# Full products written as four 32-column strips in the runs that hold value products

## The chip, the cores and the metric

The kernel runs on one core of a Trainium2 chip. Its time is the device time of that core in microseconds (us); the time before is the median of three runs. TensorE (PE in the profile) multiplies, VectorE (DVE), ScalarE (ACT) and GpSimd (POOL) work on what it leaves in PSUM and in SBUF, and SyncE (SP) issues most transfers. The profile is that of one execution.

## The reference

One input x of 2048 rows of 512 numbers goes through two branches, which a gate mixes row by row.

```python
qkv = (x @ wqkv).reshape(B, S, 3, 32, 16)           # 32 heads of 16
scores = einsum("bhqd,bhkd->bhqk", q, k) * 16 ** -0.5
mask = (i - j >= 0) & (i - j < 256)                 # a sliding window
a = (softmax(where(mask, scores, -1e9)) @ v) @ wo
b = (silu(x @ w1) * (x @ w3)) @ w2                  # F = 1376
g = sigmoid((x * gate_w).sum(-1))
out = g * a + (1 - g) * b
```

## The kernel before

TensorE's products come in three forms, by the part of the 128 x 128 array that one of them uses.

- *Full* products use 128 rows and 128 columns: the projections of q and k (`chain`, L422) and of v (`vmm`, L499), the up products of the second branch (`half`, L825, and `mm_b`, L785), its down products (`part`, L875) and the output product (`omm`, L905). A full product with 512 moving columns is the common one; those of v have 128 or 129, those of L785 have 64.
- *Row* products are the scores. A head pair's keys fill 32 of the 128 rows; four products for four row groups stand side by side (`main_batch`, L560: 8 products of 256 columns; `edge_batch`, L610: 32 products of 64 columns).
- *Column* products are the value products, in which the exponentials are multiplied by v (`pv`, L700). Each uses 128 rows and 17 columns (16 of v and one of ones for the sum); four of them write the four quarters of 32 partitions of one PSUM buffer. There are 16 blocks of them, for 4 groups of heads (c) and 4 parts of 512 query rows (w), each in two passes, and each pass needs a PSUM buffer.

PSUM holds one buffer `su` of four banks for scores and four buffers `ch_0` to `ch_3` of one bank for everything else. A buffer `ch` is free again when the instruction that reads it out is done. For the up products these are a tanh on ACT (L835) and two multiplications on DVE (L839, L845); q is copied by DVE (L480), k copied (L459) and then masked in two halves (L465) and copied once more (L462), v copied (L512) and shifted by POOL (L517). Exponentials run on ACT (L564, L614); POOL cuts their masked triangles to zero (L569, L574, L627) and DVE does part of the edge tiles (L633, L637). The result of the value products is transposed, normalised and transposed back by DVE (L724, L727, L730, L734). The down products are scaled by DVE (L880), and DVE joins both branches (L909) ahead of the output transfer (L915).

Nothing at run time chooses the order. The class `Plan` holds all operations, each with an engine, an estimated duration, the operations that it depends on, the buffers that it takes and frees, and a due time. `emit` walks them once on the host: of the engines it takes the one that can start first, and on it, among the operations that could start then, the one with the smallest rank, which is the due time. The order in which the operations leave `emit` is the order in each engine's queue, and every engine works its queue strictly in that order, waiting on semaphores. The due times come from some thirty numbers in the table `K` (L230), such as when the k projection of a part is due (`LEAD`) or the value products (`PV`).

Two parts of `emit` bear on forms. When the form of the next TensorE operation differs from the form before it, the estimated start is put back by `SWITCH` = 0.117 us. And `rank` (L70) moves due times by form: a row or column operation behind another that is not full gets 0.265 earlier (`ADJ`), a column operation behind a full one 1.114 later (`SEP`).

Of the kernel before, what the change touches and what calls it, by code (L numbers as in the profile page):

```python
# [15 lines left out]
P = 128  # L16
# [4 lines left out]

PIPE = {"DVE": 0.105, "ACT": 0.112, "POOL": 0.045}
LAT = {"PE": 0.205}
SWITCH = 0.117


class Op:
    __slots__ = ("eng", "dur", "lat", "fn", "deps", "due", "take", "free", "seq", "start", "end", "slots", "hold", "form")

    def __init__(self, eng, dur, fn, deps, due, take, free, lat, seq, form):  # L30
        self.eng, self.dur, self.fn, self.due, self.lat, self.seq = eng, dur, fn, due, lat, seq
        self.deps = [d for d in deps if d is not None]
        self.take, self.free = take, free
        self.start = self.end = None
        self.hold = 0.0
        self.form = form


class Job:
# [6 lines left out]
class Plan:  # L46


    def __init__(self, slots, beside, apart):
        self.ops = []  # L50
        self.slots = slots
        self.beside, self.apart = beside, apart

    def add(self, eng, dur, fn, deps=(), due=0.0, take=(), free=(), lat=None, form="full"):
        if lat is None:
# [5 lines left out]
    def pieces(self, cuts, each, fn, deps, due, take, lat=None, free=()):  # L61
# [4 lines left out]
                            [prev] if prev else deps, due, take=take if lo == 0 else (),  # L66
                            free=free if hi == cuts[-1] else (), lat=lat)
        return prev

    def rank(self, op, form):  # L70
        due = op.due
        if op.eng == "PE" and op.form != "full":
            if form != "full":
                due -= self.beside
            elif op.form == "column":
                due += self.apart
        return due, op.seq

    def emit(self):
        free_at = {k: [0.0] * n for k, n in self.slots.items()}  # L80
        holders = {}
        for op in self.ops:
            for job, kind in op.free:
                holders.setdefault((id(job), kind), [0, 0.0])[0] += 1
        engine = {}
        form = "full"
        todo = {}
        users = {}
        for op in self.ops:
            todo[op.seq] = len(op.deps)  # L90
            for d in op.deps:
                users.setdefault(d.seq, []).append(op)
        ready = [op for op in self.ops if not op.deps]
        order = []
        while ready:
            best = None
            lists = {}
            for op in ready:
                est = engine.get(op.eng, 0.0)
                for d in op.deps:  # L100
                    e = d.end if d.eng != op.eng else d.start + d.dur + (0.03 if op.eng in PIPE else 0.0)
# [12 lines left out]
            if first > 1e8:  # L114
                raise RuntimeError("no free buffer")
            rows = [r for r in lists[eng] if r[0] <= first + 0.001]
            held = [r for r in lists[eng] if r[1].hold and r[0] <= first + r[1].hold]
            est, op = min(held or rows, key=lambda r: self.rank(r[1], form))
            if eng == "PE" and op.form != form:
                est = max(est, engine.get(eng, 0.0) + SWITCH)  # L120
                form = op.form
            for job, kind in op.take:
                i = min(range(len(free_at[kind])), key=lambda j: free_at[kind][j])
                free_at[kind][i] = 1e9
                job.at[kind] = i
            op.start = est
            op.end = est + op.dur + op.lat + SLACK
            engine[op.eng] = est + op.dur - PIPE.get(op.eng, 0.0)
            for job, kind in op.free:
                h = holders[(id(job), kind)]  # L130
                h[0] -= 1
                h[1] = max(h[1], op.end)
                if h[0] == 0:
                    free_at[kind][job.at[kind]] = h[1]
            ready.remove(op)
            for u in users.get(op.seq, ()):
                todo[u.seq] -= 1
                if todo[u.seq] == 0:
                    ready.append(u)
            order.append((est, op))  # L140
        assert len(order) == len(self.ops)
        self.order = order
        for est, op in order:
            op.fn()


@with_exitstack
def kernel(
# [12 lines left out]
    nc = tc.nc  # L161
# [12 lines left out]
    FB = FL - FA  # L174
# [20 lines left out]
    hT = pp.tile([P, NFC - 1, 512], BF16, name="hT")  # L195
# [30 lines left out]
    ot = [pp.tile([P, D], BF16, name=f"ot_{i}") for i in range(4)]  # L226
    su = ps.tile([P, 4, 512], F32, name="su")
    ch = [ps.tile([P, 512], F32, name=f"ch_{i}") for i in range(4)]

    K = {"T0": 6.663, "TA": 234.789, "TF0": -1.359, "TF1": 251.583, "PV": 0.213, "EDGE": -2.966, "HOLD": -4.301, "LEAD": 9.863, "QLEAD": -3.864, "V": 5.26, "O0": -0.819, "O1": 5.827, "O2": 6.852, "O3": 24.592, "FE": -3.084, "PE": -2.787, "VE": -3.291, "MK": 4.4, "UP": 2.598, "_km": 1.0, "_lo": 1.0, "LE": 4.467, "ADJ": 0.265, "SEP": 1.114, "BE": -2.825}  # L230
    plan = Plan({"su": 1, "ch": 4, "Em": len(Em), "Ee": len(Ee), "kt": 2, "tt": 2, "h1": 2,
                 "tn": len(tn), "ot": len(ot), "hT": 1},
                K["ADJ"], K["SEP"])
    add = plan.add


    def half_of(base, a):
# [167 lines left out]
    def projections(c, tq):  # L405
# [13 lines left out]
        def chain(job, col, lo, hi, t0=0, t1=512):  # L419
            pst = ch[job.at["ch"]]  # L420
            for dc in range(lo, hi):
                nc.tensor.matmul(pst[:, t0:t1], lhsT=wqkv_sb[:, dc, col + c * P:col + (c + 1) * P],  # L422
                                 rhs=xT[:, dc, tq * 512 + t0:tq * 512 + t1],
                                 start=(dc == 0), stop=(dc == NDC - 1))

# [62 lines left out]
        for m0, nm in ([(4 * tq, 2), (4 * tq + 2, 2)] if c == 0 else [(4 * tq, 4)]):  # L488
# [3 lines left out]
            def vmm(lo, hi, vj=vj, m0=m0, w=w):  # L492
                pst = ch[vj.at["ch"]]
                for mm in range(lo, hi):
                    m = m0 + mm
                    for dc in range(NDC):
                        rhs = (wv0[:, dc, 0:w] if c == 0
                               else wqkv_sb[:, dc, 2 * D + c * P:2 * D + (c + 1) * P])
                        nc.tensor.matmul(pst[:, mm * w:(mm + 1) * w], lhsT=xT[:, dc, m * P:(m + 1) * P],  # L499
                                         rhs=rhs, start=(dc == 0), stop=(dc == NDC - 1))  # L500

            def v_of(rows, base, a, m0=m0, nm=nm):
# [268 lines left out]
    for tcb in range(NTC):  # L771
# [3 lines left out]
        def tail_columns(tcb=tcb):  # L775
# [4 lines left out]
            def mm_b():  # L780
                po = ch[job.at["ch"]]
                for mm in range(4):
                    m = 4 * tcb + mm
                    for dc in range(NDC):
                        nc.tensor.matmul(po[:, mm * 2 * FB:(mm + 1) * 2 * FB], lhsT=xT[:, dc, m * P:(m + 1) * P],  # L785
                                         rhs=wB[:, dc, :], start=(dc == 0), stop=(dc == NDC - 1))

            def cols(lo):
# [26 lines left out]
        for f in range(NFC):  # L815
# [6 lines left out]

            def half(job, w, lo, hi, f=f, joint=joint, tcb=tcb):
                for dc in range(lo, hi):
                    nc.tensor.matmul(ch[job.at["ch"]][:],  # L825
                                     lhsT=wA[:, dc, :] if joint else w[:, dc, f * P:(f + 1) * P],
                                     rhs=xT[:, dc, tcb * 512:(tcb + 1) * 512],
                                     start=(dc == 0), stop=(dc == NDC - 1))
# [36 lines left out]
        for mm in range(4):  # L865
# [4 lines left out]
            def part(f0, f1, job=job, mm=mm, tcb=tcb):  # L870
                bps = ch[job.at["ch"]]
                for f in range(f0, f1):
                    fs = P if f < NFC - 1 else FL
                    ht = hT[:, f] if f < NFC - 1 else hX[0:FL, tcb % 2]
                    nc.tensor.matmul(bps[:], lhsT=ht[:, mm * P:(mm + 1) * P],  # L875
                                     rhs=w2_sb[0:fs, f, :], start=(f == 0), stop=(f == NFC - 1))

            def bev(job=job, m=m):
# [18 lines left out]
    def output(m, n0, n1, queue, late):  # L897
# [4 lines left out]
        def omm(lo, hi):  # L902
            pso = ch[job.at["ch"]]
            for c in range(lo, hi):
                nc.tensor.matmul(pso[:, 0:part], lhsT=OT[:, c, m * P:(m + 1) * P], rhs=wo_sb[:, c, n0:n1],  # L905
                                 start=(c == 0), stop=(c == NDC - 1))

        def oev():
# [60 lines left out]
```

## Time and profile before

| | us |
|---|---|
| median of three runs | 240.12 (239.61 to 240.42) |
| the profiled execution, its own time | 240.56 |
| span of the profiled execution | 238.8 |
| TensorE busy (matmul rows) | 231.3 |
| DVE busy | 201.3 |
| ACT busy | 171.2 |
| POOL busy | 159.6 |

The span runs from the first instruction to the last on the core; the execution's own time holds 1.8 us more around it. A busy time is the union of an engine's rows. TensorE's rows overlap, since a product's row ends only when its result has drained, so a busy TensorE isn't TensorE at its peak: what one product costs is read from the starts of two that follow each other. A row of a group reads: line, engine, operation, what is written and read, shapes, how often; then busy us and mean ns of one; then the idle time of the engine ahead of it, and what ended it. In a timeline row the first two numbers are the start and the length, in us, of a group of like instructions that stand together. The granted clock of TensorE is 1.000 over the whole span.

### The profile page before, as it was taken

To read this page: it belongs to the slowest core of one execution; us is meant where nothing else is said; L and a number is where in the kernel's file an instruction comes from. 1 tells how busy PE (TensorE), PEld (TensorE's weight loads), DVE (VectorE), ACT (ScalarE), POOL (GpSimd) and SP (SyncE) were. 2 spreads that over 40 slices of the span, in tenths; PEclk is the share of its full clock that TensorE was granted. 3 is DMA by queue.
4 is the path that set the end of the run, shared out by engine and by line. 5 is a ranking of instruction groups with operands and counts; after the bars stand their busy time and mean duration, and the time that the engine had idled before them with its cause. 6 is when DMAs were issued, how large, how long until landed. Compare 5 with 4: busy or idle time off the path is not lost.

```text
span 238.8 us, 8528 instructions
## 1 busy us (share of the span) xinstructions
PE 231.3 (97%) x3738; PEld 118.8 (50%) x3738; DVE 201.3 (84%) x342; ACT 171.2 (72%) x141; POOL 159.6 (67%) x261
## 2 busy tenths in 40 slices
PE   8999999999999999999989899999999999999994
PEld 8554544546463543545454544545454545445442
DVE  5576998967699989996699999987899897969885
ACT  3389798876867898666858788776768989766510
POOL 7259967979857877587475777768494968575500
PEclk9999999999999999999999999999999999999999
DMA  7999980000000000000000000000000001002133
GB/s 199 205 335 276 201 212 17 5 1 3 3 3 0 5 11 11 7 0 3 3 3 3 1 8 20 3 0 3 3 3 5 3 0 25 3 22 69 52 108 110
DMA packets 20413, 11.59 MB, mean 49 GB/s; under 512 B 9656, under 2 KB 20376, under 8 KB 20376
## 3 DMA queue, kind: packets, MB, share of 16 engines
q1 hardware_dynamic: 19680, 10.59, 17.7%
q8 instruction: 29, 0.48, 0.9%
q10 hardware_dynamic: 696, 0.46, 0.6%
q14 instruction: 8, 0.07, 0.1%
HBM read 6.85 MB, written 2.10 MB: 37 GB/s over the span
## 4 chain that ended last, share of the span: by engine, by line
PE 72%; DVE 19%; ACT 4%; issue 2%; POOL 1%; DVEq 0%; ACTq 0%
PE ch L825 20%; PE ch L875 15%; PE ch L422 9%; PE ch L700 8%; PE su L560 6%; PE ch L905 5%; PE ch L499 4%; ACT Ee L614 4%; DVE h L839 3%; PE su L610 2%; DVE Ee L633 2%; DVE hT L845 2%; DVE Ee L637 2%; DVE tn L724 2%; DVE k L465 2%
## 5 line engine op out<-in xcount | busy, mean ns | idle before, releaser
L564 ACT ACTIVATE Em<-su 128x2048 bf16<-128x2048 f32 x60 | 112.6, 1877 | 34.6 <-PE su L560 31.4
L825 PE MATMUL ch<-xT,w_sb 128*128 128x512 bf16 x320 | 79.3, 380 | 0.5 <-DVE vs L512 0.3
L569 POOL TENSOR_SCALAR_AFFINE_SELECT Em<-Em 64x512 bf16<-64x512 bf16 x60 | 41.1, 685 | 32.5 <-ACT Em L564 26.9
L627 POOL TENSOR_SCALAR_AFFINE_SELECT Ee<-Ee 64x1024 bf16<-64x1024 bf16 x32 | 42.7, 1333 | 21.4 <-ACT Ee L614 19.3
L825 PEld LDWEIGHTS <-w_sb 128*128 128x128 bf16 x320 | 28.4, 98 | 34.8 <-issue 6.9
L875 PE MATMUL ch<-w_sb,hT 128*128 128x512 bf16 x160 | 40.3, 380 | 0.0
L574 POOL TENSOR_SCALAR_AFFINE_SELECT Em<-Em 64x512 bf16<-64x512 bf16 x56 | 37.3, 665 | 3.2
L614 ACT ACTIVATE Ee<-su 128x2048 bf16<-128x2048 f32 x16 | 30.0, 1876 | 10.3 <-PE su L610 7.6
L422 PE MATMUL ch<-xT,wqkv_sb 128*128 128x512 bf16 (+1 forms) x136 | 34.3, 372 | 0.0
L517 POOL COPY vs<-vs 64x256 bf16<-64x256 bf16 (+1 forms) x80 | 30.6, 382 | 5.1 <-DVE vs L512 1.8
L839 DVE SCALAR_TENSOR_TENSOR h<-tt,ch 128x512 bf16<-128x512 bf16 (+1 forms) x44 | 29.6, 677 | 4.7 <-ACT tt L835 4.5
L845 DVE SCALAR_TENSOR_TENSOR hT<-h,ch 128x512 bf16<-128x512 bf16 x40 | 27.1, 677 | 1.9
L835 ACT ACTIVATE tt<-ch 128x512 bf16<-128x512 f32 (+1 forms) x44 | 25.7, 594 | 2.4 <-PE ch L825 2.2
L700 PEld LDWEIGHTS <-vs 128*17 128x17 bf16 x1664 | 21.1, 92 | 8.6 <-issue 6.3
L700 PE MATMUL ch<-Em,vs 128*17 128x256 bf16 (+2 forms) x672 | 22.9, 242 | 2.4 <-DVE h L839 1.7
L700 PE MATMUL ch<-Ee,vs 128*17 128x64 bf16 x992 | 22.6, 193 | 0.0
L875 PEld LDWEIGHTS <-hT 128*128 128x128 bf16 x160 | 13.9, 98 | 16.8 <-issue 3.2
L422 PEld LDWEIGHTS <-wqkv_sb 128*128 128x128 bf16 x136 | 12.4, 99 | 12.7 <-issue 2.1
L499 PEld LDWEIGHTS <-xT 128*128 128x128 bf16 x256 | 15.8, 97 | 5.6 <-issue 1.8
L880 DVE TENSOR_SCALAR bsb<-ch,omg 128x512 bf16<-128x512 f32 x15 | 11.2, 747 | 7.6 <-PE ch L875 7.4
L560 PE MATMUL su<-qT,kz 32*128 32x256 bf16 x240 | 17.3, 278 | 0.2
L560 PE MATMUL su<-qT,k 32*128 32x256 bf16 x240 | 16.7, 268 | 0.0
(81 smaller groups left out, 257.4 us busy)
## 6 DMA issues: line engine op xcount, KB each, us to landing
out_dram<-ot SPq DMA_DIRECT2D x15, 128.0 KB, 1.7
wqkv_sb<-in_A_wqkv_dram SPq DMA_DIRECT2D x5, 256.0 KB, 5.7
w_sb<-in_B_w_dram SPq DMA_DIRECT2D x1, 1280.0 KB, 6.7
w_sb<-in_B_w_dram SPq DMA_DIRECT2D x2, 608.0 KB, 7.8
w_sb<-in_B_w_dram SPq DMA_DIRECT2D x2, 512.0 KB, 5.2
w_sb<-in_B_w_dram SPq DMA_DIRECT2D x2, 256.0 KB, 4.9
wo_sb<-in_A_wo_dram SPq DMA_DIRECT2D x1, 512.0 KB, 5.5
xs<-in_A_x_dram SPq DMA_DIRECT2D x1, 256.0 KB, 2.9
```

The costliest lines, as they stand in the source:

```text
L422: nc.tensor.matmul(pst[:, t0:t1], lhsT=wqkv_sb[:, dc, col + c * P:col + (c + 1) * P], rhs=xT[:, dc, tq * 512 + t0:tq * 512 + t1], start=(d ...
L560: nc.tensor.matmul(su[:, s, a * 256:(a + 1) * 256], lhsT=head_keys(r, t, a), rhs=qT[r, q0:q0 + 256], start=True, stop=True)
L564: nc.scalar.activation(out=Em[job.at["Em"]][:], in_=su[:].rearrange("p s (a q) -> p s a q", a=2), func=ACT.Exp, scale=SCALE)
L569: nc.gpsimd.affine_select(out=e, in_=e, pattern=[[0, 8], [1, KB]], compare_op=ALU.is_ge, fill=0.0, base=0, channel_multiplier=-1)
L574: nc.gpsimd.affine_select(out=e, in_=e, pattern=[[0, 8], [-1, KB]], compare_op=ALU.is_ge, fill=0.0, base=-1, channel_multiplier=1)
L614: nc.scalar.activation(out=Ee[ej.at["Ee"]][:].rearrange("p s t k q -> p s (t k q)"), in_=su[:], func=ACT.Exp, scale=SCALE)
L627: nc.gpsimd.affine_select(out=e, in_=e, pattern=[[0, 4], [0, 4], [1, KB]], compare_op=ALU.is_ge, fill=0.0, base=0, channel_multiplier=-1)
L700: nc.tensor.matmul(po[32 * s:32 * s + VW, lo - 512 * w:hi - 512 * w], lhsT=vs[:, i, a * VW:(a + 1) * VW], rhs=mov, start=(n == 0), stop=(n ...
L825: nc.tensor.matmul(ch[job.at["ch"]][:], lhsT=wA[:, dc, :] if joint else w[:, dc, f * P:(f + 1) * P], rhs=xT[:, dc, tcb * 512:(tcb + 1) * 512],
L839: nc.vector.scalar_tensor_tensor(out=h1[job.at["h1"]][ru, :], in0=tt[job.at["tt"]][rg, :], scalar=1.0, in1=ch[job.at["ch"]][rg, :], op0=AL ...
L845: nc.vector.scalar_tensor_tensor(out=dst, in0=h1[job.at["h1"]][ru, :], scalar=0.5, in1=ch[up.at["ch"]][ru, :], op0=ALU.mult, op1=ALU.mult)
L875: nc.tensor.matmul(bps[:], lhsT=ht[:, mm * P:(mm + 1) * P], rhs=w2_sb[0:fs, f, :], start=(f == 0), stop=(f == NFC - 1))
```

## The change

Every full product that the plan issues, transposes apart, goes through a new function `product`, which writes it in one of two ways.

```diff
+    def product(out, lhsT, rhs, start, stop):
+        if not plan.strips:
+            nc.tensor.matmul(out, lhsT=lhsT, rhs=rhs, start=start, stop=stop)
+            return
+        for j in range(0, P, 32):
+            nc.tensor.matmul(out[j:j + 32], lhsT=lhsT[:, j:j + 32], rhs=rhs, start=start, stop=stop)
```

Where `plan.strips` is set, the 128 columns of the weights are cut into four strips of 32; each strip multiplies the same moving columns and writes a quarter of the partitions. Which operations are written so is decided after the order is known: TensorE's operations are cut into runs between row operations, and every operation of a run that holds a column operation is marked.

```diff
+        run = []
+        for op in [op for est, op in order if op.eng == "PE"] + [None]:
+            if op and op.form != "row":
+                run.append(op)
+                continue
+            column = any(o.form == "column" for o in run)
+            for o in run:
+                o.strips = column
+            run = []
         for est, op in order:
+            self.strips = op.strips
             op.fn()
```

The order is computed anew as well. A change of form is charged only where one side is a row operation, at 0.125 instead of 0.117 us; `rank` and its two numbers are gone; and the numbers of `K` are others.

```diff
-SWITCH = 0.117
+SWITCH = 0.125
...
-            est, op = min(held or rows, key=lambda r: self.rank(r[1], form))
-            if eng == "PE" and op.form != form:
-                est = max(est, engine.get(eng, 0.0) + SWITCH)
+            est, op = min(held or rows, key=lambda r: (r[1].due, r[1].seq))
+            if eng == "PE":
+                if op.form != form and "row" in (op.form, form):
+                    est = max(est, engine.get(eng, 0.0) + SWITCH)
                 form = op.form
...
-    K = {"T0": 6.663, "TA": 234.789, "TF0": -1.359, "TF1": 251.583, "PV": 0.213, "EDGE": -2.966, "HOLD": -4.301, "LEAD": 9.863, "QLEAD": -3.864, "V": 5.26, "O0": -0.819, "O1": 5.827, "O2": 6.852, "O3": 24.592, "FE": -3.084, "PE": -2.787, "VE": -3.291, "MK": 4.4, "UP": 2.598, "_km": 1.0, "_lo": 1.0, "LE": 4.467, "ADJ": 0.265, "SEP": 1.114, "BE": -2.825}
+    K = {"T0": 6.766, "TA": 235.106, "TF0": -1.288, "TF1": 251.005, "PV": 0.365, "EDGE": -3.423, "HOLD": -4.941, "LEAD": 10.494, "QLEAD": -3.881, "V": 6.91, "O0": -1.457, "O1": 6.08, "O2": 6.573, "O3": 24.217, "FE": -2.851, "PE": -2.787, "VE": -3.545, "MK": 5.885, "UP": 2.958, "_km": 1.0, "_lo": 1.0, "LE": 5.367, "BE": -3.541}
```

The products at L422, L499, L785, L825, L875 and L905 call `product` in place of `nc.tensor.matmul`, with the same arguments. In the program that results, 214 full products are written as strips and 822 as before. Instructions that other engines execute are the same in number and kind, in another order.

More of the change, by code (lines that the diff above doesn't have):

```diff
@@ L23 @@
 LAT = {"PE": 0.205}
-SWITCH = 0.117
+SWITCH = 0.125
 class Op:
-    __slots__ = ("eng", "dur", "lat", "fn", "deps", "due", "take", "free", "seq", "start", "end", "slots", "hold", "form")
+    __slots__ = ("eng", "dur", "lat", "fn", "deps", "due", "take", "free", "seq", "start", "end", "slots", "hold", "form", "strips")
     def __init__(self, eng, dur, fn, deps, due, take, free, lat, seq, form):
@@ L36, in __init__ @@
         self.form = form
+        self.strips = False
 class Job:
@@ L46, with __init__ @@
 class Plan:
-    def __init__(self, slots, beside, apart):
+    def __init__(self, slots):
         self.ops = []
         self.slots = slots
-        self.beside, self.apart = beside, apart
+        self.strips = False
     def add(self, eng, dur, fn, deps=(), due=0.0, take=(), free=(), lat=None, form="full"):
@@ L68, in pieces @@
         return prev
[L70 to L77, printed above, removed]
     def emit(self):
@@ L228 @@
     ch = [ps.tile([P, 512], F32, name=f"ch_{i}") for i in range(4)]
-    K = {"T0": 6.663, "TA": 234.789, "TF0": -1.359, "TF1": 251.583, "PV": 0.213, "EDGE": -2.966, "HOLD": -4.301, "LEAD": 9.863, "QLEAD": -3.864, "V": 5.26, "O0": -0.819, "O1": 5.827, "O2": 6.852, "O3": 24.592, "FE": -3.084, "PE": -2.787, "VE": -3.291, "MK": 4.4, "UP": 2.598, "_km": 1.0, "_lo": 1.0, "LE": 4.467, "ADJ": 0.265, "SEP": 1.114, "BE": -2.825}
+    K = {"T0": 6.766, "TA": 235.106, "TF0": -1.288, "TF1": 251.005, "PV": 0.365, "EDGE": -3.423, "HOLD": -4.941, "LEAD": 10.494, "QLEAD": -3.881, "V": 6.91, "O0": -1.457, "O1": 6.08, "O2": 6.573, "O3": 24.217, "FE": -2.851, "PE": -2.787, "VE": -3.545, "MK": 5.885, "UP": 2.958, "_km": 1.0, "_lo": 1.0, "LE": 5.367, "BE": -3.541}
     plan = Plan({"su": 1, "ch": 4, "Em": len(Em), "Ee": len(Ee), "kt": 2, "tt": 2, "h1": 2,
-                 "tn": len(tn), "ot": len(ot), "hT": 1},
-                K["ADJ"], K["SEP"])
+                 "tn": len(tn), "ot": len(ot), "hT": 1})
     add = plan.add
+    def product(out, lhsT, rhs, start, stop):
[4 more added lines that the diff above has]
+            nc.tensor.matmul(out[j:j + 32], lhsT=lhsT[:, j:j + 32], rhs=rhs, start=start, stop=stop)
     def half_of(base, a):
@@ L421, in chain @@
             for dc in range(lo, hi):
-                nc.tensor.matmul(pst[:, t0:t1], lhsT=wqkv_sb[:, dc, col + c * P:col + (c + 1) * P],
+                product(pst[:, t0:t1], lhsT=wqkv_sb[:, dc, col + c * P:col + (c + 1) * P],
                                  rhs=xT[:, dc, tq * 512 + t0:tq * 512 + t1],
@@ L498, in vmm @@
                                else wqkv_sb[:, dc, 2 * D + c * P:2 * D + (c + 1) * P])
-                        nc.tensor.matmul(pst[:, mm * w:(mm + 1) * w], lhsT=xT[:, dc, m * P:(m + 1) * P],
+                        product(pst[:, mm * w:(mm + 1) * w], lhsT=xT[:, dc, m * P:(m + 1) * P],
                                          rhs=rhs, start=(dc == 0), stop=(dc == NDC - 1))
@@ L784, in mm_b @@
                     for dc in range(NDC):
-                        nc.tensor.matmul(po[:, mm * 2 * FB:(mm + 1) * 2 * FB], lhsT=xT[:, dc, m * P:(m + 1) * P],
+                        product(po[:, mm * 2 * FB:(mm + 1) * 2 * FB], lhsT=xT[:, dc, m * P:(m + 1) * P],
                                          rhs=wB[:, dc, :], start=(dc == 0), stop=(dc == NDC - 1))
@@ L824, in half @@
                 for dc in range(lo, hi):
-                    nc.tensor.matmul(ch[job.at["ch"]][:],
+                    product(ch[job.at["ch"]][:],
                                      lhsT=wA[:, dc, :] if joint else w[:, dc, f * P:(f + 1) * P],
@@ L874, in part @@
                     ht = hT[:, f] if f < NFC - 1 else hX[0:FL, tcb % 2]
-                    nc.tensor.matmul(bps[:], lhsT=ht[:, mm * P:(mm + 1) * P],
+                    product(bps[:], lhsT=ht[:, mm * P:(mm + 1) * P],
                                      rhs=w2_sb[0:fs, f, :], start=(f == 0), stop=(f == NFC - 1))
@@ L904, in omm @@
             for c in range(lo, hi):
-                nc.tensor.matmul(pso[:, 0:part], lhsT=OT[:, c, m * P:(m + 1) * P], rhs=wo_sb[:, c, n0:n1],
+                product(pso[:, 0:part], lhsT=OT[:, c, m * P:(m + 1) * P], rhs=wo_sb[:, c, n0:n1],
                                  start=(c == 0), stop=(c == NDC - 1))
```

## The prediction

> **What bounds the kernel now.** First the page: busy shares and the chain that ended last.
>
> ```profile
> span 238.8 us, 8528 instructions
> PE 231.3 (97%) x3738; PEld 118.8 (50%) x3738; DVE 201.3 (84%) x342; ACT 171.2 (72%) x141; POOL 159.6 (67%) x261
> PE 72%; DVE 19%; ACT 4%; issue 2%; POOL 1%; DVEq 0%; ACTq 0%
> ```
>
> TensorE is occupied almost throughout and carries 72% of the chain; DVE carries the next 19%. Next the list of waits, for TensorE alone: us in total, times, longest.
>
> ```profile
> PE ch L700 <- DVE h L839: 1.7, 2, 0.9
> PE su L296 <- DVE warm L299: 1.1, 1, 1.1
> PE ch L700 <- DVE hT L845: 0.5, 1, 0.5
> PE ch L825 <- DVE vs L512: 0.3, 1, 0.3
> ...
> ```
>
> Three more waits of 0.2 follow (L499, L825, and L700 on L909). Without the opening (L296) the list sums to 3.1 us, all of it a PSUM buffer `ch` that a DVE instruction has not yet given back. Asked by stretch, 2.7 of the 3.1 (all but the L499 and L909 lines) lie between 72 and 149 us. The busy table by stretches says why: columns are PE, PEld, DVE, ACT, POOL.
>
> ```profile
> 122.00:149.00 27.00, 26.12 (x430) 13.00 (x418) 26.24 (x42) 21.22 (x18) 18.50 (x27) 1.00 0.04 8
> 149.00:200.00 51.00, 50.91 (x892) 26.18 (x891) 45.52 (x78) 39.69 (x30) 35.63 (x52) 1.00 0.02 4
> ```
>
> In the middle DVE is busy 26.24 of 27 us and TensorE loses 0.88; after 149 TensorE loses 0.09 of 51. So time taken off TensorE counts in full after 149, and competes with DVE between 72 and 149. The granted clock is 1.00 in both rows.
>
> What a change of form costs does not show as a wait; it is read from starts in TensorE's timeline.
>
> ```profile
> 65.67 1.46 PE L825 MATMUL ch<-xT,w_sb 128*128 128x512 bf16 x6
> 67.06 0.21 PE L700 MATMUL ch<-Em,vs 128*17 128x64 bf16 x4
> 67.09 0.20 PE L700 MATMUL ch<-Ee,vs 128*17 128x64 bf16 x4
> 67.12 0.26 PE L700 MATMUL ch<-Em,vs 128*17 128x192 bf16 x4
> ...
> 67.74 0.20 PE L700 MATMUL ch<-Em,vs 128*17 128x64 bf16 x4
> ...
> 68.33 0.26 PE L700 MATMUL ch<-Ee,vs 128*17 128x64 bf16 x12
> 68.52 0.29 PE L560 MATMUL su<-qT,kz 32*128 32x256 bf16 x4
> 68.64 0.28 PE L560 MATMUL su<-qT,k 32*128 32x256 bf16 x4
> 68.85 0.61 PE L825 MATMUL ch<-xT,w_sb 128*128 128x512 bf16 x2
> ```
>
> A full 512-column product takes 0.216 us from start to start (ten from 229.65 to 231.81). The six from 65.67 end their slots at 66.96, the value products start at 67.06: 0.10 for full to column. The row quad at 68.64 streams 0.107, to 68.75; the full product starts at 68.85: 0.10 again. Column to row: the three quads from 68.33 take 0.087, to 68.42, and the row form starts at 68.52, 0.10. Full to row, read likewise elsewhere, also gives 0.10.
>
> **The change, part by part.**
>
> *Form changes.* Counted in the instruction orders of the two programs. Before: 62 full to row, 76 row to full, 16 full to column, 2 column to full, 14 column to row: 170. After, with strips and value products as one form: 60 full to row, 59 row to full, 17 into strips or columns from row, 16 back: 152. 18 fewer x 0.10 = **-1.8 us**. No row shows row to strip; the other changes all read 0.10 to 0.12, which moves the sum by 0.3 at most (33 x 0.01). By place: 4 of the 18 fall before 72, 7 between 72 and 149, 7 later.
>
> *Strips.* 214 full products become 856 strip products: 122 with 512 moving columns, 8 with 256, 84 value projections (V) with 128 or 129. Loads and matmuls each rise by 642. If four strips ran one after another, each 512 product would take 0.85 us; the value products exclude it, since four of them over 64 columns take 0.03 together (67.06, 67.09, 67.12). A whole pass, 67.06 to 67.74, is 14 quads with 1,536 columns in 0.68 us. One column takes 0.2133/512 = 0.417 ns by the full product less some 2.7 ns, so 1,536 take 0.640 and a quad adds 2.9 ns, like a full product. Lower end: 214 products at the old price, 0. Upper end: the 0.04 of the pass grows with columns instead of quads, 13 ns in 512, so 122 x 10 ns = 1.2, with the V products 1.4. I take **+0.3**, near the per-quad reading, with something for loads 32 columns wide that no row shows.
>
> The extra instructions cost issue and fetch: four loads and four matmuls per 0.029 us already run in the value products, and a strip product has 0.056 (V: sixteen from 69.29 to 70.18) or 0.216. The DMA share of 0.02 to 0.04 after 72 hides the fetch. DVE, ACT, POOL and SP issue as many instructions as before; they are only re-ordered.
>
> *The first value products move.* In the order before, eight V products (L499) stand ahead of them; after, they do not, and the value products come first. Timeline of all engines before:
>
> ```profile
> 27.33 0.62 PE L499 MATMUL ch<-wv,xT 128*128 128x129 bf16 x8 [0.22 <-DVE h L839]
> 27.66 0.65 POOL L574 TENSOR_SCALAR_AFFINE_SELECT Em<-Em 64x512 bf16<-64x512 bf16 x1
> 27.93 0.29 PE L700 MATMUL ch<-Em,vs 128*17 128x256 bf16 x4
> 28.38 0.20 PE L700 MATMUL ch<-Em,vs 128*17 128x64 bf16 x4
> ```
>
> The quad at 28.38 reads the tile that the POOL select finishes at 28.31. After, the same buffer comes free at 27.33, the 0.42 of quads ahead of that one end at 27.75, and TensorE stands until 28.38: **+0.6**, with the eight V products (0.45) still to do. Behind it on TensorE's queue wait the second pass, then the scores that feed ACT. Lower end -0.2, if the new order brings the select forward and the old 0.22 wait goes; upper end 1.0, if POOL is later by a copy (L517, 0.3 to 0.4).
>
> *The DVE-bound stretch.* The 7 changes saved between 72 and 149 are 0.7 us. DVE, at 91% (21.09, 22.51 and 26.24 us busy in the three stretches to 95, 122 and 149, 69.8 of 77), is what the `ch` buffers wait for; TensorE arriving earlier waits longer. I give them back whole: **+0.7**. Lower end -2.7 (the new order also loses the stretch's old waits), upper end +1.8 (two of the encounters below). The 4 before 72 I keep, since DVE itself stood 0.62 us for TensorE's L422 at 116.8 and moves forward with it.
>
> **Sum:** -1.8 + 0.3 + 0.6 + 0.7 = **-0.2 us** on the profiled execution (240.56 us, span 238.8, 1.8 around it; the last product to the end is unchanged). That execution is 0.44 above the median, 240.12, so the forecast is **239.9**.
>
> **Rivals.**
>
> *Faster: the orders' waits come to nothing.* The +0.6 and +0.7 do not appear; -1.8 + 0.3 = -1.5, **238.6**. For it: after 149, with 7 changes, nothing but TensorE limits; the order is wholly new, and may place its value products where buffers are free. Against: the first block, whose order I could follow instruction by instruction.
>
> *Slower: key copies meet POOL selects.* Place: DVE's masked-key and edge copies between 72 and 149.
>
> ```profile
> 119.72 1.24 DVE L462 COPY kz<-k 128x512 bf16<-128x512 bf16 x1
> 120.88 0.67 DVE L839 SCALAR_TENSOR_TENSOR h<-tt,ch 128x512 bf16<-128x512 bf16 x1
> ```
>
> L462 takes 0.40 on average and 1.24 here, beside POOL's L627 (118.12 to 120.81); its successor L839 ends at 121.55 and TensorE, idle 0.89, starts at 121.60. One such encounter costs 0.9. The new order shuffles them; two more in the stretch give -0.2 + 1.8 = +1.6, **241.7**. It decides from the first additional one on (+0.7). For it: 24 L465 and 12 L462 are exposed. Against: it may as well remove one.
>
> *The change does not do what it says.* Strips of 32 columns and value products of 17 still drain between each other. 17 strip-to-column and 7 column-to-strip borders x 0.1 = +2.4, together +2.2: **242.3**. No row shows such a border. Against: both forms use the same 32-partition quarters of the output.
>
> *Weight loads fall behind.* A load's own row is 92 to 98 ns. If one stayed exposed in each V strip product: 84 x (92 - 56) = +3.0, **242.9**. Against: 4 x 17 weight columns go through in a 29 ns quad, 2.3 a nanosecond; 128 then need 55 ns and a V product lasts 56.
> [...]
>
> **How the numbers follow.** About 0.3% (0.7 us) is what a measurement of this kernel can tell from no change. Forecast, 239.4 to 240.8: 0.43. Waits come to nothing: 0.27. Encounters: 0.22. Drain between strips: 0.05. Loads: 0.03. Hence faster 0.27, same 0.43, slower 0.30. The range, 238.2 to 242.0, reaches below the faster rival, to half a microsecond of the old waits gone as well, and above the second encounter. It leaves out the rest of the old waits, which could bring 235.9 only if the order lost them all, a third encounter, and the two last rivals: under 0.2 together.
>
> **What would show it.** Right: no 0.1 us hole between strips and value products; a 512 strip product at 0.216 to 0.219 from first strip to first strip; about 152 holes of 0.1; a TensorE wait of some 0.6 us on POOL L574's successor near 28; between 72 and 149 TensorE waits of 3 to 4 us on DVE. Wrong: strips spaced over 0.225; holes at their borders; waits on DVE after 149, where I assume none; or a sum of TensorE waits below 2 or above 6 us.

## The result, and the profile after

The changed kernel takes 241.81 us (240.71 to 242.57, eleven executions), the kernel before, timed beside it, 240.30 (239.34 to 241.11): a ratio of 1.0058, 95% interval 1.0035 to 1.0081. It is slower by about 1.4 us where I had forecast no change, inside the range but on the other side. The profiled execution took 240.91 us, which is low among its own. Two executions of the comparisons below stand far outside the others, one of the kernel before with 451.6 us and one of experiment 2 with 377.83 us at a granted clock of 0.56, and no ratio holds them.

The page of the changed kernel (busy time; the queues that carry instructions; the chain that ended last). In this kernel a full product is L240, a strip L243, a value product L709, and the score batches are L569 and L619.

```profile
span 239.2 us, 9782 instructions
PE 226.3 (95%) x4347; PEld 120.6 (50%) x4380; DVE 199.6 (83%) x342; ACT 171.2 (72%) x141; POOL 160.0 (67%) x261
...
q8 instruction: 34, 0.56, 1.0%
...
PE 67%; DVE 18%; issue 5%; DMA 4%; POOL 2%; SPq 1%; ACT 1%; DVEq 0%; ACTq 0%
```

The same queue on the page of before (packets, MB, share):

```profile
q8 instruction: 29, 0.48, 0.9%
```

DVE, ACT and POOL do what they did. The chain gives 5% to "issue", time in which an engine waited for nothing that the profile shows, where before it had 2%. The instruction queue moves five packets more. Both counts go by TensorE's instructions: 7,487 before and 8,773 after, at 256 to a packet (1,286 more for five packets more; the holes below stand whole multiples of 256 apart), are 29.2 and 34.3.

TensorE's waits after (us in total, times, longest):

```profile
PE ch L240 <- issue: 4.0, 18, 1.3
...
PE ch L709 <- DVE h L848: 1.1, 2, 0.9
PE su L569 <- issue: 0.5, 1, 0.5
PE ch L243 <- DVE hT L854: 0.5, 1, 0.5
PE ch L709 <- POOL Ee L636: 0.3, 1, 0.3
```

The waits on other engines did not grow: with three more of 0.2 to 0.3 on DVE and one of 0.2 on a transfer they sum to 2.9 us without the opening, before to 3.1. Between 72 and 149 us, where I had placed the growth, they are 1.2 us (0.9 on L848, 0.3 on L854), before 2.7. New are the long lines of "issue". The 4.0 needs care: 4,347 matmul rows stand for 4,380 weight loads, so 33 rows are missing, and a missing 512-column product reads as an idle 0.2. Read from the weight loads, which are complete, three holes are real: 29.40 to 30.93, 43.42 to 44.21 and 111.55 to 111.87 us (the last from the product at 111.55). Less the ordinary spacing they cost 1.48, 0.69 and 0.30, together 2.47 us.

The two stretches of the prediction (columns PE, PEld, DVE, ACT, POOL):

```profile
122.00:149.00 27.00, 25.70 (x506) 12.77 (x498) 26.18 (x42) 21.10 (x20) 19.04 (x28) 1.00 0.04 8
149.00:200.00 51.00, 49.43 (x1043) 27.05 (x1044) 46.07 (x79) 39.70 (x31) 36.08 (x52) 1.00 0.02 5
```

DVE is as full as before in the middle, and the DMA share, on which I had leaned, did not move: 0.04 and 0.02.

TensorE's timeline after, at the first two holes and in the closing strips:

```profile
28.69 0.64 PE L240 MATMUL ch<-wB,xT 128*128 128x64 bf16 x16
29.16 0.45 PE L240 MATMUL ch<-wv,xT 128*128 128x129 bf16 x5
30.93 0.33 PE L240 MATMUL ch<-wv,xT 128*128 128x129 bf16 x3 [1.31 <-issue]
...
41.49 0.64 PE L243 MATMUL ch<-wv,xT 128*32 128x129 bf16 x32
41.95 0.20 PE L709 MATMUL ch<-Em,vs 128*17 128x64 bf16 x4
...
43.41 0.29 PE L569 MATMUL su<-qT,kz 32*128 32x256 bf16 x4
44.21 0.29 PE L569 MATMUL su<-qT,k 32*128 32x256 bf16 x4 [0.52 <-issue]
...
229.07 2.34 PE L243 MATMUL ch<-w_sb,hT 128*32 128x512 bf16 x40
231.23 0.40 PE L243 MATMUL ch<-w_sb,hX 96*32 96x512 bf16 x4
```

The first hole splits eight like products, 5 and 3, of which none waits for another engine; the second splits one score batch. No buffer and no operand is late there. What the strips were to do, they did: 32 strips of a V projection from 41.49 are eight products at 0.056, which end at 41.94, and the value products start at 41.95 with no hole; 40 strips from 229.07 to 231.23 are ten products at 0.216.

Each hole stands at one place of TensorE's instruction stream: before instruction 707, 1,219 and 3,779 (one off at most, since what is seen is the next load or product that starts), which are 195 plus 256 times 2, 4 and 14. In the trace's rows of the instruction queue a packet starts at 28.49, 41.82 and 109.50 us, and TensorE goes on 2.44, 2.39 and 2.37 us after it. My first reading was therefore: TensorE's stream arrives in blocks of 256 instructions, the transfer of the next block starts about when TensorE enters the one ahead, and a block that is used up in less than some 3 us leaves TensorE standing. The largest hole is not behind such a block: the one ahead of 29.40 lasted 3.7 us, but the packet started 2.8 us after TensorE had entered it, while the inputs were still loading (272 GB/s from 28 to 29 us). The value passes use instructions fastest (14 quads, 112 instructions, in 0.68 us), and a strip product has eight instructions where a full one has two. Before, no block lasted under 3.6 us; after, the shortest lasts 1.7.

### The profile page after: what moved, and what is told of

Read it like the earlier page. It is cut to its first block, busy times and chain, and to the rows that moved or that the text cites. A ratio compares the mean times of both kernels' runs of the same rounds, so it can differ in the third digit from the quotient of the medians.

```text
span 239.2 us, 9782 instructions
## 1 busy us (share of the span) xinstructions
PE 226.3 (95%) x4347; PEld 120.6 (50%) x4380; DVE 199.6 (83%) x342; ACT 171.2 (72%) x141; POOL 160.0 (67%) x261
## 4 chain that ended last, share of the span: by engine, by line
PE 67%; DVE 18%; issue 5%; DMA 4%; POOL 2%; SPq 1%; ACT 1%; DVEq 0%; ACTq 0%
PE ch L240 41%; PE ch L243 10%; PE ch L709 8%; PE su L569 6%; DVE h L848 3%; DVE hT L854 2%; DMA xT<-in_A_x_dram 2%; DVE Ee L642 2%; PE su L619 2%; DMA wqkv_sb<-in_A_wqkv_dram 2%; DVE kz L471 1%; DVE kt L468 1%; DVE k L474 1%; DVE tn L733 1%; SPq L294 1%
## 5 line engine op out<-in xcount | busy, mean ns | idle before, releaser
L240 PE MATMUL ch<-xT,w_sb 128*128 128x512 bf16 x264 | 66.2, 380 | 1.7 <-issue 1.1
L240 PEld LDWEIGHTS <-w_sb 128*128 128x128 bf16 x279 | 24.9, 98 | 30.0 <-issue 4.5
L583 POOL TENSOR_SCALAR_AFFINE_SELECT Em<-Em 64x512 bf16<-64x512 bf16 x56 | 37.2, 664 | 3.3
L848 DVE SCALAR_TENSOR_TENSOR h<-tt,ch 128x512 bf16<-128x512 bf16 (+1 forms) x44 | 29.4, 675 | 4.5 <-ACT tt L844 4.1
L240 PE MATMUL ch<-w_sb,hT 128*128 128x512 bf16 x125 | 32.0, 380 | 0.9 <-issue 0.8
L240 PE MATMUL ch<-xT,wqkv_sb 128*128 128x512 bf16 (+1 forms) x123 | 30.6, 366 | 1.0 <-issue 0.5
L854 DVE SCALAR_TENSOR_TENSOR hT<-h,ch 128x512 bf16<-128x512 bf16 x40 | 27.0, 674 | 2.6 <-PE ch L240 1.1
L709 PEld LDWEIGHTS <-vs 128*17 128x17 bf16 x1664 | 22.6, 92 | 6.4 <-issue 2.4
L709 PE MATMUL ch<-Em,vs 128*17 128x256 bf16 (+2 forms) x672 | 23.3, 242 | 1.5 <-DVE h L848 1.1
L709 PE MATMUL ch<-Ee,vs 128*17 128x64 bf16 x992 | 23.1, 193 | 0.5 <-POOL Ee L636 0.3
L240 PEld LDWEIGHTS <-hT 128*128 128x128 bf16 x132 | 11.6, 98 | 13.7 <-issue 1.9
L240 PEld LDWEIGHTS <-wqkv_sb 128*128 128x128 bf16 x131 | 11.9, 98 | 11.7 <-issue 0.8
L569 PE MATMUL su<-qT,kz 32*128 32x256 bf16 x240 | 17.3, 278 | 0.0
L569 PE MATMUL su<-qT,k 32*128 32x256 bf16 x240 | 16.7, 268 | 0.5 <-issue 0.5
L240 PEld LDWEIGHTS <-xT 128*128 128x128 bf16 x236 | 12.8, 98 | 6.3 <-issue 3.2
```

The costliest lines, as they stand in the source:

```text
L240: nc.tensor.matmul(out, lhsT=lhsT, rhs=rhs, start=start, stop=stop)
L569: nc.tensor.matmul(su[:, s, a * 256:(a + 1) * 256], lhsT=head_keys(r, t, a), rhs=qT[r, q0:q0 + 256], start=True, stop=True)
L583: nc.gpsimd.affine_select(out=e, in_=e, pattern=[[0, 8], [-1, KB]], compare_op=ALU.is_ge, fill=0.0, base=-1, channel_multiplier=1)
L709: nc.tensor.matmul(po[32 * s:32 * s + VW, lo - 512 * w:hi - 512 * w], lhsT=vs[:, i, a * VW:(a + 1) * VW], rhs=mov, start=(n == 0), stop=(n ...
L848: nc.vector.scalar_tensor_tensor(out=h1[job.at["h1"]][ru, :], in0=tt[job.at["tt"]][rg, :], scalar=1.0, in1=ch[job.at["ch"]][rg, :], op0=AL ...
L854: nc.vector.scalar_tensor_tensor(out=dst, in0=h1[job.at["h1"]][ru, :], scalar=0.5, in1=ch[up.at["ch"]][ru, :], op0=ALU.mult, op1=ALU.mult)
```

## The experiments

The rival readings were: the new order is worse; strips cost more than full products or stall on something of their own; the first value block waits (my +0.6); or the block borders. The kernel before, with which all are compared, had medians of 240.16 in the first set and 240.08 in the second.

**1. The new order without strips.** Edit, in the changed kernel:

```diff
-                o.strips = column
+                o.strips = False
```

> The new order with no strips: every full product is one instruction pair again, so TensorE has 642 pairs fewer and 24 changes of form more (17 full to column, 7 column to full, 0.1 us each, +2.4). Theory of the instruction blocks (TensorE's instructions come in blocks of 256; a block can be used about 2.4 us after its transfer starts, and where 256 instructions are used up sooner TensorE stands still): the three holes of the changed kernel at such borders (1.48, 0.69 and 0.30 us near 29, 43 and 112 us) go, -2.5, so about 241.7, or 241.0 where DVE's waits take some of the changes in. Rival, the new order's waits on DVE are what made it slower: the waits stay and the changes come on top, 243.5 to 244.2.

Measured: 240.49 us (240.31 to 242.01), ratio 1.0024 (1.0005 to 1.0043). My two figures, 241.7 and 241.0, were too high by 0.5 and more; which of their terms was wrong is not shown. Its waits on "issue" are single missing rows of 0.2, or 0.3 with a change of form, and one hole:

```profile
PE ch L240 <- issue: 2.9, 18, 0.2
...
30.79 0.27 PE L569 MATMUL su<-qT,k 32*128 32x256 bf16 x2
31.26 0.28 PE L569 MATMUL su<-qT,k 32*128 32x256 bf16 x2 [0.20 <-issue]
```

A quad of a score batch is split after two of its products and goes on 0.46 later, at instruction 707: the border that has the first hole of the changed kernel is late without strips too, 2.5 us after its packet's start, which was 3.1 us after TensorE had entered the block ahead. The other two holes are gone.

So the order alone is nearly the kernel before, although it has 176 changes of form, 24 more than the changed kernel. With strips those 24 go, and the time rises by 1.3 us. The loss lies with the strips, not with the order.

**2. Strips in the order before.** Edit: `product` and the marking of runs as in the change, everything else as before.

> The order before, with full products in runs that hold value products written as strips: 183 products, 549 instruction pairs more, 152 changes of form instead of 170 (-1.8). Counting instructions along the times of the profile before, the shortest blocks of 256 are then used up in 2.24 us (near 54), 2.43 (66), 2.54 (162), 2.57 (40) and 2.69 (174), where before none took less than 3.6. Theory of the instruction blocks: holes at those places that wait for nothing the profile shows, 0.3 us in all if each transfer starts at once, 4 us if each starts 0.9 late; 238.9 to 242.4. Rival, the new order's waits: the order is the old one, so no new wait, 238.5, or 239.2 where DVE takes back the seven changes between 72 and 149 us.

Measured: 245.69, 246.33 and 244.40 us, ratio 1.0212 (1.0154 to 1.027), with 18 changes fewer. My range had ended at 242.4: it allowed for 4 us of holes, but not for what the clock adds. The waits of its profile:

```profile
PE ch L720 <- issue: 2.7, 3, 1.9
...
PE su L580 <- issue: 0.8, 1, 0.8
```

Here the first hole lies inside the value products and lasts 2.02 us (29.14 to 31.18); three more, at 59.95, 168.75 and 181.26, have 0.62, 0.95 and 0.57. All four stand at 195 plus a multiple of 256 again. And the granted clock (third number from the end) falls behind the long one:

```profile
30.00:31.00 1.00, 0.00 (x0) 0.00 (x0) 0.00 (x0) 0.00 (x0) 0.90 (x3) 1.00 0.51 110
31.00:32.00 1.00, 0.81 (x17) 0.57 (x18) 0.57 (x1) 0.23 (x1) 0.76 (x3) 0.84 1.15 299
32.00:33.00 1.00, 1.00 (x14) 0.72 (x13) 1.00 (x6) 1.00 (x1) 0.00 (x0) 0.50 1.12 343
33.00:34.00 1.00, 0.78 (x3) 0.35 (x3) 0.83 (x3) 0.81 (x2) 0.29 (x1) 0.50 1.19 298
34.00:35.00 1.00, 1.00 (x3) 0.30 (x2) 1.00 (x4) 0.00 (x0) 0.95 (x2) 0.50 1.20 291
35.00:36.00 1.00, 1.00 (x12) 0.33 (x11) 0.52 (x1) 0.24 (x1) 0.07 (x1) 0.96 0.51 121
```

From 31 to 36 the missing clock is 0.16 + 0.50 + 0.50 + 0.50 + 0.04 = 1.7 us. Laid over the trace of before, product by product, it is 0.1 behind at 27 us. With holes of 4.2 and the clock's 1.7 that makes 6.0 us; at the end it is 5.1 behind, so 0.9 of the 1.8 has been saved. The span is 244.0 against 238.8.

**3. The same, but the first run with value products left full.** Edit, on the kernel of 2:

```diff
+        seen = 0
...
             column = any(o.form == "column" for o in run)
+            seen += column
             for o in run:
-                o.strips = column
+                o.strips = column and seen > 1
```

> As the kernel of the order before with strips, but the first run that holds value products stays in full products: 39 pairs fewer, one change of form more (+0.1), and every later block of 256 instructions begins 78 instructions later. By the same count the shortest block is then 3.09 us (223), the next 4.16. Theory of the instruction blocks: no holes, 238.6, or 239.3 where DVE takes back the seven changes between 72 and 149; faster than its sibling by what that one loses in holes. Rival: 0.1 slower than its sibling.

Measured: **239.50 us** (239.12 to 240.18), ratio 0.9967 (0.9955 to 0.998): faster than both kernels, with 170 products in strips. The 39 pairs of load and matmul fewer move every later border by 78 instructions, and no border has a hole. Since the order is that of before, the two traces can be laid over each other. TensorE's waits on DVE, before:

```profile
94.98 0.21 PE L700 MATMUL ch<-Em,vs 128*17 128x64 bf16 x4 [0.55 <-DVE hT L845]
121.60 0.21 PE L700 MATMUL ch<-Em,vs 128*17 128x64 bf16 x4 [0.89 <-DVE h L839]
135.73 0.29 PE L700 MATMUL ch<-Em,vs 128*17 128x256 bf16 x4 [0.76 <-DVE h L839]
225.97 0.21 PE L700 MATMUL ch<-Em,vs 128*17 128x64 bf16 x4 [0.16 <-DVE ot L909]
```

and in this kernel:

```profile
94.42 0.21 PE L722 MATMUL ch<-Em,vs 128*17 128x64 bf16 x4 [0.55 <-DVE hT L867]
120.93 0.21 PE L722 MATMUL ch<-Em,vs 128*17 128x64 bf16 x4 [0.88 <-DVE h L861]
135.06 0.29 PE L722 MATMUL ch<-Em,vs 128*17 128x256 bf16 x4 [0.76 <-DVE h L861]
224.83 0.21 PE L722 MATMUL ch<-Em,vs 128*17 128x64 bf16 x4 [0.26 <-DVE ot L931]
```

It is 0.56 us ahead at the first, 0.67 at the next two and 1.14 at the last. Of the 0.56, 0.24 come from an earlier start of the products near 6 us, which varies between executions. The starts of the same weight loads show the steps. At the value block of 81 us the lead grows from 0.58 to 0.68, and by 86.5 it is 0.58 again. The blocks of 95, 121 and 135 begin with a wait on DVE, and the change that is saved there only lengthens the wait. From 72 to 149 us the lead grows by 0.1 in all, for seven changes. Behind 149 no wait takes it back: 0.66 at 149, then 0.76 at the block of 163, 0.94 at 189, 1.04 at 202, 1.14 at 216 and 1.24 at 225, of which the last wait, on `ot`, keeps 0.1.

**4. What a block costs by itself.** Edit: the kernel before, with quads of idle products behind the plan, of 17 weight columns with 64 and 256 moving columns, then strips with 512.

```diff
+        for quads, cols, n in ((512, VW, 64), (256, VW, 256), (128, 32, 512)):
+            for i in range(quads):
+                for s in range(4):
+                    nc.tensor.matmul(su[32 * s:32 * s + cols, 0, 0:n], lhsT=w2_sb[:, i % 8, 32 * s:32 * s + cols],
+                                     rhs=w2_sb[:, 8, 0:n], start=True, stop=True)
```

> The kernel before, with products behind its end whose results nobody reads: 512 quads of 17 columns with 64 moving columns (256 instructions are 32 quads, 0.93 us of work), then 256 quads with 256 moving columns (3.5 us a block), then 128 quads of 32 columns with 512 (6.9 us a block). Theory of the instruction blocks: the first part stands still at every 32nd quad and takes 2.4 us or more a block, about 40 us instead of 15; the second runs at 0.110 a quad with short holes or none; the third at 0.216 a quad. Rival, instructions are always there: 0.029, 0.110 and 0.216 us a quad throughout, 71 us in all.

Measured, in TensorE's timeline (the start, the length, what, how many):

```profile
258.69 1.89 PE L942 MATMUL su<-w_sb 128*17 128x64 bf16 x128 [2.12 <-issue]
262.69 1.89 PE L942 MATMUL su<-w_sb 128*17 128x64 bf16 x128 [2.12 <-issue]
266.42 1.89 PE L942 MATMUL su<-w_sb 128*17 128x64 bf16 x128 [1.84 <-issue]
...
301.89 3.67 PE L942 MATMUL su<-w_sb 128*17 128x256 bf16 x128 [0.33 <-issue]
...
313.63 40.45 PE L942 MATMUL su<-w_sb 128*17 128x256 bf16 x957 [0.33 <-issue]
```

Products that wait for nothing run 128 at a time, with their loads 256 instructions, and then stand. A block starts every 3.45 to 4.0 us, however short its work. With 256 columns a block holds about 3.5 us of work and the idle is 0.33 or nothing; with 512 there is none. So here a block has to last 3.5 to 4 us. The first part took some 62 us, where I had expected about 40: I had counted 2.4 us a block. The whole kernel took 356.69 us in its one execution, and its granted clock was 0.55 in the first part.

**5. The changed kernel, its stream moved by 54 instructions.** This is the test of place. The warm-up products ahead of the work are split in two, and nothing of the work changes:

```diff
-    def warm_up(n):
-        for i in range(n):
-            nc.tensor.matmul(su[:, 0, 0:P], lhsT=warm[:], rhs=warm[:], start=True, stop=True)
+    def warm_up(n, cols=P):
+        for i in range(n * P // cols):
+            nc.tensor.matmul(su[:, 0, 0:cols], lhsT=warm[:], rhs=warm[:, 0:cols], start=True, stop=True)
...
-        warm_up(WARM)
+        warm_up(WARM, P // 2)
```

> The changed kernel with its 27 warm-up products written as 54 of half the width: every TensorE instruction of the real work moves 54 places back in the stream, and nothing else changes. If the holes belong to borders between blocks of 256 instructions, they leave their places: none at the products that stood at 43.4 and 111.6 us. The borders now fall near 22.8, 28.4, 39.4, 41.5, 52.7, 55 and 172.4 us on the work's old clock; the short blocks are those that begin at 39.4 (2.1 us of work, hole at its end up to 1.2), 52.7 (2.7, up to 0.6) and 172.4 (2.6, up to 0.7), and the hole of 29.4 moves to 28.4 with 1 to 2.5 us, since its transfer still stands behind the input loads. Time 240.5 to 243.0. If the holes belong to the work (strips that wait on an operand, or a port), they stay at the same three products with 1.5, 0.7 and 0.3 us, and the time is the changed kernel's, 241.8 within 0.5.

Measured: **239.88 us** (239.07 to 240.61), ratio to before 0.9988 (0.9971 to 1.0006). The changed kernel itself, in the same set, took 241.68 (experiment 8). The same work with 27 products more ahead of it is 1.8 us faster, and below the 240.5 to 243.0 that I had expected. Laid over each other, the two traces are still within 0.05 us of each other at 13.8 us, so the gain is not in the opening. The timeline of the moved kernel:

```profile
28.77 0.64 PE L240 MATMUL ch<-wB,xT 128*128 128x64 bf16 x16
29.25 0.63 PE L240 MATMUL ch<-wv,xT 128*128 128x129 bf16 x8
...
41.95 0.19 PE L709 MATMUL ch<-Ee,vs 128*17 128x64 bf16 x1
42.71 0.23 PE L709 MATMUL ch<-Ee,vs 128*17 128x64 bf16 x7 [0.57 <-issue]
...
43.05 0.29 PE L569 MATMUL su<-qT,kz 32*128 32x256 bf16 x4
43.17 0.28 PE L569 MATMUL su<-qT,k 32*128 32x256 bf16 x4
```

The eight V products that the first hole had split run through. The hole of the score batch at 43.4 now stands among value products at 41.95, 27 products earlier, at instruction 1,219 once more; that of 111.6 is gone, and a small one (0.3) has appeared at 176.2 in a score batch, at instruction 6,595. Together they are 1.0 us, against 2.5. The part on record that failed is the first hole, which I had given 1 to 2.5 us at its new place: the border at 28.4 has none. Its transfer started at 25.83, 3.0 us after TensorE had entered the block ahead, and the block lasts 5.6.

**6. The changed kernel with its first such run left full** (the edit of 3 on the changed kernel; 30 instructions fewer).

> The changed kernel with its first run of full products that holds value products left unsplit: 30 instructions fewer from about 26 us on. If the block borders cause the holes, the border that stood at 29.4 comes after the dense part, near 31, and the hole of 1.48 goes; short blocks remain near 40.5 (2.9 us), 54 (2.9), 92.6 (2.8), 107.6 (2.5), 119 (2.8), 132.7 (2.4) and 222 (2.6), each with a hole of 0 to 0.9. Time 239.8 to 241.0, below the changed kernel by 0.8 to 2. If the first block's delay is the wait for the select, as I predicted, the hole stays and the time stays at 241.8 within 0.5.

Measured: 239.60 us (239.19 to 240.66), ratio 0.9976 (0.9959 to 0.9993), just under my range. The border that had stood in the V products came to 31.2 and has no hole. The short blocks that I had listed cost little, though their packets were seldom early (the one for 111.6 started at 109.26, 2.4 us before): read from the starts of products, the borders near 43.9, 57.8, 96.8 and 111.6 have holes of 0.26, 0.13, 0.1 and 0.1, some 0.6 us in all.

**7. Strips only in the last six runs, after 149 us,** in the order before (`seen > 10` in the edit of 3).

> The order of before, with strips only in the six last runs that hold value products, all after 149 us: 7 form changes fewer, 282 instructions fewer than all runs would have, one short block near 174 us (2.6 us of work). If a change saved after 149 counts in full and only there: 240.2 - 0.7 = 239.5, up to 240.1 if the short block gives a hole of 0.6. No hole before 149, and the waits up to 149 us as in before within 0.1. If the gain of the kernel with all runs but the first lay in the opening or in chance, this one takes 240.2 within 0.3.

Measured: 239.92 us (239.45 to 241.09), ratio 0.999 (0.9973 to 1.0007). That lies in both of my ranges, so the time alone decides nothing; the trace shows more. (The kernel has 267 pairs of load and product fewer than that of experiment 2, and 282 more than before, which is the number that I had given.) The short block was where the count had put it:

```profile
176.45 0.27 PE L722 MATMUL ch<-Ee,vs 128*17 128x64 bf16 x11
177.40 0.19 PE L722 MATMUL ch<-Ee,vs 128*17 128x64 bf16 x1 [0.69 <-issue]
```

The hole costs 0.86, more than the 0.6 that I had allowed. Laid over before, the trace is 0.24 behind at 149 us, from its opening, and 0.06 at the block of 176. Behind the hole it is 0.82 behind at the value block of 189, then 0.73, 0.62 and 0.52 at those of 202, 216 and 225: a tenth comes back at every block, and in this execution, the slowest of its twelve (241.09), the one hole costs more than the seven changes earn.

**8. The changed kernel again, four more profiles.** No edit; the question was why its median stands 0.9 above its profiled execution.

> The changed kernel once more, for the size of its holes and the granted clock behind them in another profile. By the block borders: holes at the same three places (29.4, 43.4, 111.6), their sizes free to vary by the start of the transfer, about 0 to 2.5 us for the first; a first hole of 2 us or more is followed by a lowered granted clock, one of 1.5 is not. Median 241.5 to 242.2. If the holes were a chance of one execution, they are elsewhere or absent and the time is again spread without them.

> The changed kernel, one further profile. The profiles so far lie low among its times (240.91 and 241.24 us where the medians are 241.8 and 241.7). If the slower executions are slower by longer holes, then one of 241.7 or more shows the three holes (29.4, 43.4, 111.6 us) with a sum of 3.3 us or more, against 2.5 at 240.91 and 2.8 at 241.24, with the granted clock at 1.00. If they are slower by something else (the opening, or waits on DVE), the sum stays at 2.4 to 2.9.

> As the look before: by longer holes, time and the sum of the three holes rise together, about 1 us for each 1.3 us of holes (by the pair of profiles with and without them: 1.0 us of span for 1.5 to 1.7 us of holes); by another cause, the sum stays at 2.4 to 2.9 whatever the time.

> As the two looks before, for a further point of the time against the sum of the holes.

The first of these was timed too: 241.68 us (240.52 to 242.21), ratio 1.0047 (1.0022 to 1.0073). The holes, with the first profile:

| profiled execution, us | first hole | second | third | sum | other |
|---|---|---|---|---|---|
| 240.84 | 1.52 | 0.67 | 0.2 | 2.4 | |
| 240.91 | 1.48 | 0.69 | 0.30 | 2.5 | |
| 241.24 | 1.27 | 0.98 | 0.52 | 2.8 | |
| 242.51 | 1.69 | 0.96 | 0.27 | 2.9 | opening later by 1.1 |
| 242.76 | 2.21 | 0.65 | 0.28 | 3.1 | clock at half after the first |

The places never change, the sizes do. Longer holes alone, my expectation, explain less than half of the spread. In 242.51 the first value products start at 28.22 where they start at 27.15 in 240.91, a delay that has nothing to do with the change. In 242.76 the first hole is over 2 us, and the clock falls (windows of that execution, granted clock third from the end):

```profile
32.00:34.00 2.00, 2.00 (x13) 0.50 (x12) 1.40 (x3) 0.00 (x0) 0.00 (x0) 0.52 1.18 300
34.00:36.00 2.00, 2.00 (x7) 0.69 (x7) 0.93 (x6) 1.98 (x2) 1.21 (x5) 0.63 0.54 129
36.00:40.00 4.00, 4.00 (x56) 1.68 (x54) 2.97 (x5) 3.05 (x4) 1.75 (x3) 1.00 0.10 20
```

That is 2 x 0.48 + 2 x 0.37 = 1.7 us of clock for a hole that was 0.7 longer.

## Why the prediction was wrong

**The step that failed** reads: "The extra instructions cost issue and fetch: four loads and four matmuls per 0.029 us already run in the value products [...] The DMA share of 0.02 to 0.04 after 72 hides the fetch." I costed the fetch as bandwidth, at nothing, and named an idle DMA as its cover. What it costs is the time from a packet's start to the use of its instructions: in the 25 holes of more than 0.1 us at borders in all these runs but the probe, TensorE goes on 2.35 to 2.82 us after its packet's start, and packets start between 1.8 us before and 1.8 us after TensorE passes the border ahead (up to 4.1 after it while the inputs load). The cover is the time that 256 instructions last, and the change shortened that cover beside the value products, where it was thinnest, and at 29 us, where the packet was late. That those already run at eight instructions in 0.029 us was no evidence for the strips: it was the reason why a run of both is too fast. The term is +2.5 us in the profiled execution, up to 3.1, with the clock's 1.7 on top in the execution whose first hole lasted 2.21. Moving the stream by 54 instructions takes 1.8 us off the median.

**The other terms**, in the order of the sum:

- *Changes of form, -1.8:* right. A change between strips and value products took 2 to 3 ns more than the stream (17 and 7 borders, less two where TensorE waits for a buffer), any other 0.10 to 0.12 us. No drain between strips and columns: that rival is out.
- *Strips, +0.3:* too high. Products of 512 columns keep 0.216, of 128 columns 0.056, as full products do. Weight loads do not fall behind: that rival is out too.
- *The first value products, +0.6:* nothing. This is a second step that failed, and it had a dependency that isn't there. The quad that I had waiting for the POOL select starts at 27.60, while that select runs from 27.48 to 28.13 (rows below): the select writes the last 64 of the 256 columns of the tile (L583), and the quad reads the first 64. TensorE waits 0.18 at 27.15 for the first pass's buffer, where before it waited 0.22, and 0.09 at 27.74 for the second's, which the copy of q (L489) gives back at 27.69; before, it stood 0.08 at that place, behind L845.
- *The DVE-bound stretch, +0.7:* right for the order of before, as experiment 3 shows step by step: seven changes between 72 and 149 us leave 0.1, those after 149 leave 0.6. For the new order it is not shown. The waits of 3 to 4 us on DVE there, which I had named as a sign, are 1.2 us in the changed kernel and 2.4 in that of experiment 6.

The rows of the first value block after the change:

```profile
27.01 0.68 DVE L489 CAST qT<-ch 128x512 bf16<-128x512 f32 x1
27.48 0.65 POOL L583 TENSOR_SCALAR_AFFINE_SELECT Em<-Em 64x512 bf16<-64x512 bf16 x1
27.60 0.20 PE L709 MATMUL ch<-Em,vs 128*17 128x64 bf16 x4
...
27.74 0.29 PE L709 MATMUL ch<-Em,vs 128*17 128x256 bf16 x4
```

Without holes the sum would have been -1.8 + 0.7 = -1.1, a median of 239.0 to 239.2 by the medians of before (240.12 and 240.30). The changed kernel with its first run full took 239.60 with 0.6 us of holes, and the moved one 239.88 with 1.0; less their holes, these are 239.0 and 238.9. With 2.5 us of holes the sum gives 241.7 by the median beside it, and 241.81 was measured, but such agreement is loose: by the two profiled executions it would be 240.56 + 1.4 = 242.0 against 240.91. Openings differ by up to 1.1 us, and part of a hole can come back: laid over the moved kernel, the profile of the changed one falls back by 1.4 at its first hole and regains 0.3 by 33 us.

**The rivals.** "Key copies meet POOL selects" gave 241.7, almost the number measured, for a reason that isn't there: the waits on DVE did not grow. It shows how little a right number proves. "The orders' waits come to nothing" was true of the first value block, and the waits between 72 and 149 us did fall; the holes hid it.

## What to carry to other kernels

When an edit multiplies instructions on an engine, count instructions per microsecond in the densest stretch, not only busy time or DMA share: here, once the inputs were in, a block of 256 that TensorE used up in 1.7 to 2.9 us cost up to 1.0 us or nothing, and none of 3.0 us or more cost anything (in experiment 4 one of 3.5 us still cost 0.33); while the inputs were loading, blocks of 3.1 to 5.0 us cost 0.5 to 2.2. A hole with no releaser that splits like instructions and keeps its index in the stream, not its place in the work, was such a border here (before instructions 707, 1,219 and 3,779); moving the stream by 54 instructions ahead of the work, or leaving the first run unsplit, tested it and took most of it away (1.0 and 0.6 us of holes are left, of 2.5). What the edit then saved counted only behind the last wait of the stretch: in the order of before, a tenth per block after 149 us and almost nothing between 72 and 149.

## What the runs showed of the hardware

- TensorE's instructions arrived in packets of 256 (29 packets for 7,487 instructions before, 34 for 8,773 after; the holes of the changed kernel and of experiment 2 stand at 195 plus a multiple of 256), and the next packet's transfer started about when the border ahead of it was passed, most often within 1.2 us after it (1.8 us before it at the earliest, once the inputs were in). In the 25 holes outside experiment 4, its first instruction was used 2.35 to 2.82 us after that start. What sets the start of a transfer within these bounds was not found; that the first one is late because of the input loads is likely from its place, and was not tried.
- A TensorE hole of 2.02 us (experiment 2) and one of 2.21 us (the execution of 242.76 us) were followed by some 3 to 4 us at about half the granted clock (0.50 from 32 to 35 us in the one; 0.52 and 0.63 in the two windows from 32 to 36 us in the other), worth 1.7 us; holes of up to 1.69 us in the changed kernel were not.
- Four strips of 32 weight columns side by side cost what a full product cost (0.216 us for 512 moving columns, 0.056 for 128), and a change from them to 17-column products cost 2 to 3 ns where a change to row products cost 0.10 us.
